# First batch's score limits moved from VectorE to ScalarE, and key splits moved from ScalarE to GpSimd

## The chip, the core and the metric

The kernel runs on one core of a Trainium2 chip. The metric is the device time of one execution in microseconds; the number for the kernel before is the median of three runs. A profiled execution has a span (first to last instruction) and a time of its own, slightly longer.

## What is computed

Three layers follow each other: attention with a threshold, a channel-mixing MLP, and a mixture of experts. Only the first and the start of the second are touched.

```python
scores = scale * np.matmul(q, k.transpose(0, 1, 3, 2))        # 4 batches, 8 heads, 576 x 576, head size 64
thresh = np.max(scores, axis=-1, keepdims=True) - tau
scores = np.where(scores >= thresh, scores, -1000000000.0)
attn = np.exp(scores - np.max(scores, axis=-1, keepdims=True))
attn = attn / (np.sum(attn, axis=-1, keepdims=True) + 1e-09)
x = np.matmul(attn, v)                                        # then: h = x^T U V, u = x + h^T, relu(u w1) w2, experts
```

## The kernel before, in words

**Stages.** Batch 0's attention runs alone (`attention_alone(0)`), beside it only the conversion of the MLP's weights (`convert`), which reads them in 512-column pieces. After it comes a loop over batches 1 to 3, in which the attention of batch b is interleaved with the MLP (`channel`) of batch b - 1. The last MLP and the experts follow.

**Attention.** Two heads are one pair; a batch has four pairs, numbered over all batches i = 4b + hp. A pair has five groups of 128 query rows: four with two score tiles (one for each head) and a fifth with one, so nine score tiles of 128 x 576 in a pair and 36 in a batch. For each score tile the steps are: `scores` (TensorE, four matmuls into a PSUM tile `s`, of which there are two), `peak` (VectorE, the negated row maximum into column 0 of `st`), `exp` (ScalarE, reads `s`, writes `p`), `limits` (column 1 of `st` = row maximum - tau: the lowest score that is kept) and `mask` (VectorE, sets to zero what lies below the limit, and adds up the row in the same instruction). `mask` is the last reader of `s`. Then `back` transposes `p` on TensorE, ScalarE copies the transposed blocks to `ptt`, and matmuls with `v` follow.

**Keys.** Matmuls are done with a high and a low part of each operand. `load_pair` loads a pair's keys in two pieces (576 and 640 columns) into `raw` buffers, of which there are three; `kh` is the rounded copy and `kl` = raw - `kh`. Until now `kh` is always made by ScalarE; `kl` is made by GpSimd (`eng` is `pool`) for pairs 1 to 7 and by VectorE otherwise. A pair's load is issued one pair ahead.

**Order.** Each engine works through its own instructions in order. A scheduler places them, except that GpSimd's stand in the order written while batch 0 runs. SP issues the loads and stores, also in order. `t8` holds the constants from `tau`.

Of the kernel before, what the change touches and what calls it, by code (L numbers as in the profile page):

```python
# [14 lines left out]
AF = mybir.ActivationFunctionType  # L15
ALU = mybir.AluOpType
# [87 lines left out]
def attention_channel_moe(ctx, tc, qk, vv, tau, umat, vrep, wch, wgl, wexp, consts, out):  # L104
    nc = tc.nc
    pe, dve, act, pool, sp = nc.tensor, nc.vector, nc.scalar, nc.gpsimd, nc.sync
# [10 lines left out]
    t8 = cp.tile([128, 4], F32, name="t8")  # L117
# [135 lines left out]
    def scalars():  # L253

        sp.dma_start(out=t8[:, 0:1], in_=tau)

        dve.tensor_scalar(out=t8[:, 1:2], in0=t8[:, 0:1], scalar1=NEGTAU, scalar2=0.125, op0=ALU.is_ge, op1=ALU.mult)
        dve.tensor_scalar(out=t8[:, 2:3], in0=t8[:, 1:2], scalar1=0.0, scalar2=BIG, op0=ALU.is_equal, op1=ALU.mult)
        dve.tensor_scalar(out=t8[:, 0:1], in0=t8[:, 0:1], scalar1=0.0, scalar2=t8[:, 2:3], op0=ALU.max, op1=ALU.add)

    def load_pair(b, hp, later=None):

        i = b * NPAIR + hp
        v = ap.tile([128, VW], F32, tag="v", name=f"v{i}")
        qs = ap.tile([128, QKW], F32R, tag="qs", name=f"qs{i}")
        kh = ap.tile([128, QKW], F32R, tag="kh", name=f"kh{i}")
        kl = ap.tile([128, QKW], F32R, tag="kl", name=f"kl{i}")

        cuts = ((0, 0, 128), (1, 0, S), (0, 704, 832), (1, S, QKW), (0, 128, 704), (0, 832, QKW)) if i == 0 else (
            (1, 0, S), (1, S, QKW), (0, 0, 608), (0, 608, QKW))  # L270
        eng = dve if i == 0 or b > 1 else pool
        def steps():
            for n, (kq, c0, c1) in enumerate(cuts):
                c = slice(c0, c1)
                nm = f"raw{i}_{n}"
                if (i, n) == (0, 1):
                    x = mlp.tile([128, S], F32, tag="yr", name=nm, bufs=2)
                elif i == 0 and c1 - c0 == 128:
                    x = mlp.tile([128, 512], F32, tag="wr", name=nm, bufs=WR)
                else:  # L280
                    x = ap.tile([128, 640], F32, tag="raw", name=nm, bufs=3)
                x = x[:, :c1 - c0]
                sp.dma_start(out=x, in_=qk[i][:, kq, c])
                if (i, n) == (0, 0):
                    scalars()
                if (i, n) == (0, 3):
                    sp.dma_start(out=cst, in_=consts)
                if kq:
                    act.activation(kh[:, c], x, AF.Copy)
                    eng.tensor_tensor(out=kl[:, c], in0=x, in1=kh[:, c].bitcast(F32), op=ALU.subtract)  # L290
                else:
                    act.activation(qs[:, c], x, AF.Copy, scale=t8[:, 1:2])
                    lo, hi, xl = qs[64:128, c], qs[64:128, c].bitcast(F32), x[64:128]
                    dve.scalar_tensor_tensor(out=lo, in0=xl, scalar=t8[64:128, 1:2], in1=hi,
                                             op0=ALU.mult, op1=ALU.subtract)
                yield
            sp.dma_start(out=v, in_=vv[i])

        if later is None:
            for _ in steps():  # L300
                pass
        else:
            later.append(steps())
        return qs, kh, kl, v
# [13 lines left out]
    class Group:  # L318
# [30 lines left out]

        def limits(self, c0, c1):  # L350

            dve.tensor_scalar(out=self.st[:, 1, c0:c1], in0=self.st[:, 0, c0:c1], scalar1=-1.0, scalar2=t8[:, 0:1],
                              op0=ALU.mult, op1=ALU.subtract)

        def halves(self, h):
            return self.pt[:, h].rearrange("p (a b) -> p a b", a=2)
# [1018 lines left out]
```

## Time and profile before

| | us |
|---|---|
| median of 3 runs | 1030.57 (1028.63 to 1031.76) |
| the profiled execution | 1029.61 |
| its span | 1027.8 |
| TensorE busy | 995.2 (97%) |
| VectorE busy | 719.3 (70%) |
| ScalarE busy | 611.8 (60%) |
| GpSimd busy | 152.2 (15%) |

Busy shares are means over all stages. In batch 0's attention alone (up to about 101 us) the shares are others than later, so that stage has to be read by itself. The granted clock of the profiled core was 0.996 over the span.

### The profile page before, as it was taken

How to read it: one execution, taken by the hardware profiler on the slowest of the kernel's cores; microseconds unless marked ns; L12 is line 12 of the kernel's file. 1: busy time of each engine (PE TensorE's matmuls, PEld its weight loads, DVE VectorE, ACT ScalarE, POOL GpSimd, SP SyncE). 2: the span in 40 equal slices, each digit the busy share in tenths (PEclk: the TensorE clock that was granted, in tenths of full speed). 3: DMA queues.
4: the chain of work that ended last, by engine and by line, in shares of the span. 5: the costliest groups of instructions: out<-in, count | busy, mean ns of one | idle time of the engine just before them, and what ended most of it. 6: DMA issues, size and time to landing. Idle time of an engine off the chain costs nothing. (4 is left out here: it accounts for less than half of the span.)

```text
span 1027.8 us, 17859 instructions
## 1 busy us (share of the span) xinstructions
PE 995.2 (97%) x6352; PEld 836.2 (81%) x6352; DVE 719.3 (70%) x1761; ACT 611.8 (60%) x1242; POOL 152.2 (15%) x143
## 2 busy tenths in 40 slices
PE   7898999989999999999999999999999999999996
PEld 4666677768787787788889898999998998889984
DVE  7998697776778877877676664683369755566673
ACT  6888777776677777776565653422354444455562
POOL 1332245342000000000000000013400321120100
PEclk9999999999999999999999999999999999999998
DMA  6655577864323322423121110453055555566550
GB/s 213 220 153 162 160 257 245 273 209 140 116 92 94 125 72 83 127 90 94 55 68 42 42 43 31 139 207 122 25 192 180 177 202 185 174 192 198 196 184 16
DMA packets 58241, 143.72 MB, mean 140 GB/s; under 512 B 7389, under 2 KB 8157, under 8 KB 58144
## 3 DMA queue, kind: packets, MB, share of 16 engines
q1 hardware_dynamic: 54784, 132.27, 40.0%
q0 software_dynamic: 3360, 10.23, 3.1%
q8 instruction: 52, 0.85, 0.3%
q14 instruction: 45, 0.37, 0.1%
HBM read 124.65 MB, written 18.61 MB: 139 GB/s over the span
## 5 line engine op out<-in xcount | busy, mean ns | idle before, releaser
L1125 ACT ACTIVATE eh<-ew 128x512 fp32r<-128x512 f32 x160 | 94.2, 628 | 68.1 <-PE el L1241 47.7
L1126 DVE TENSOR_TENSOR el<-ew,eh 128x512 fp32r<-128x512 f32 x160 | 106.7, 692 | 37.7 <-ACT eh L1125 36.2
L702 PE MATMUL l<-uh,w0h 128*128 128x256 f32 (+2 forms) x352 | 127.0, 361 | 0.3 <-ACT yT L508 0.3
L363 DVE SCALAR_TENSOR_TENSOR p<-s,st,p 128x576 f32<-128x576 f32 x144 | 114.1, 814 | 15.8 <-ACT p L359 12.4
L359 ACT ACTIVATE p<-s,st 128x576 f32<-128x576 f32 x144 | 103.7, 738 | 33.1 <-DVE st L348 31.6
L703 PE MATMUL l<-ul,w0h 128*128 128x256 f32 (+2 forms) x352 | 122.6, 348 | 0.0
L704 PE MATMUL l<-uh,w0l 128*128 128x256 f32 (+2 forms) x352 | 122.3, 348 | 0.0
L348 DVE TENSOR_REDUCE st<-s 128x1 f32<-128x576 f32 x144 | 105.1, 749 | 18.0 <-PE s L315 17.4
L717 PE MATMUL l<-hh,w1h 128*128 128x512 f32 (+3 forms) x320 | 115.2, 360 | 0.0
L719 PE MATMUL l<-hh,w1l 128*128 128x512 f32 (+3 forms) x320 | 112.8, 353 | 0.0
L718 PE MATMUL l<-hl,w1h 128*128 128x512 f32 (+3 forms) x320 | 112.2, 351 | 0.0
L417 ACT ACTIVATE ptt<-tp 128x512 f32<-128x512 f32 (+1 forms) x192 | 88.4, 490 | 30.1 <-PE tp L416 30.0
L313 PE MATMUL s<-kh,qs 128*128 128x288 f32 x320 | 95.5, 318 | 5.6 <-DVE p L363 3.6
L681 POOL TENSOR_TENSOR w1l<-wr,w1h 128x512 fp32r<-128x512 f32 x24 | 31.7, 1333 | 457.5 <-DVE rha L984 426.6
L416 PE MATMUL tp<-cst,p 128*128 128x128 f32 x576 | 90.8, 276 | 5.2 <-ACT ptt L417 5.0
L722 DVE TENSOR_TENSOR yT<-l,yT 128x448 f32<-128x448 f32 (+2 forms) x96 | 50.0, 521 | 57.9 <-PE l L719 57.5
L315 PE MATMUL s<-kl,qs 128*128 128x288 f32 x320 | 88.5, 296 | 0.0
L373 ACT ACTIVATE p<-p,rv 128x576 f32<-128x576 f32 x108 | 78.6, 771 | 15.3 <-DVE rv L380 15.0
L416 PEld LDWEIGHTS tp<-cst,p 128*128 128x128 f32 x576 | 67.8, 140 | 20.6 <-ACT ptt L417 11.4
L313 PEld LDWEIGHTS s<-kh,qs 128*128 128x128 f32 x320 | 60.3, 188 | 15.6 <-DVE p L363 6.4
L435 PE MATMUL po<-ptt,v 128*64 128x256 f32 (+1 forms) x256 | 69.8, 413 | 2.4 <-ACT ptt L424 1.5
L706 DVE SCALAR_TENSOR_TENSOR hl<-l,hh 128x512 fp32r<-128x512 f32 (+2 forms) x80 | 46.3, 578 | 36.7 <-ACT hh L705 36.4
(604 smaller groups left out, 2468.6 us busy)
## 6 DMA issues: line engine op xcount, KB each, us to landing
ew<-in_wexp_dram SPq DMA_DIRECT2D x80, 512.0 KB, 4.6
wr<-wdram SPq DMA_DIRECT2D x128, 256.0 KB, 3.1
cr<-in_wch_dram SPq DMA_DIRECT2D x32, 512.0 KB, 5.2
raw<-in_qk_dram SPq DMA_DIRECT2D x30, 304.0 KB, 3.2
wdram<-w SPq DMA_DIRECT2D x32, 256.0 KB, 3.0
v<-in_vv_dram SPq DMA_DIRECT2D x16, 352.0 KB, 3.9
raw<-in_qk_dram SPq DMA_DIRECT2D x16, 320.0 KB, 3.8
raw<-in_qk_dram SPq DMA_DIRECT2D x17, 288.0 KB, 3.0
```

What stands on the lines that cost most here:

```text
L313: pe.matmul(s["t"][:, h, :288], lhsT=qs[:, qc:qc + 128], rhs=kh[:, k0:k0 + 288], start=(j == 0), stop=False)
L348: dve.tensor_reduce(out=self.st[:, 0, h:h + 1], in_=self.t[h], axis=AX.XY, op=ALU.max, negate=True)
L359: act.activation(self.halves(h), self.t[h], AF.Exp, bias=self.st[:, 0, h:h + 1])
L363: dve.scalar_tensor_tensor(out=p, in0=self.t[h], scalar=self.st[:, 1, h:h + 1], in1=p, op0=ALU.is_ge, op1=ALU.mult, accum_out=self.rvs[:, ...
L416: pe.transpose(tp[:, c - c0], src[:, c * 128:c * 128 + 128], ident)
L702: pe.matmul(pm, lhsT=w1h[:, wk], rhs=uh[k], start=(k == 0), stop=False)
L703: pe.matmul(pm, lhsT=w1h[:, wk], rhs=ul[k], start=False, stop=False)
L704: pe.matmul(pm, lhsT=w1l[:, wk], rhs=uh[k], start=False, stop=(k == 3))
L717: pe.matmul(pm, lhsT=w2h[:, wd], rhs=xh, start=(f == f0), stop=False)
L718: pe.matmul(pm, lhsT=w2h[:, wd], rhs=xl, start=False, stop=False)
L719: pe.matmul(pm, lhsT=w2l[:, wd], rhs=xh, start=False, stop=(f == f0 + 3))
L1126: dve.tensor_tensor(out=lo, in0=x, in1=hi.bitcast(F32), op=ALU.subtract)
```

## The change

Two edits. In batch 0, `limits` is one ScalarE instruction for each score tile (36 in all) in place of one on VectorE; it needs -tau as a bias, which one more VectorE instruction writes to `t8` at the start. And where `kl` is made by GpSimd (pairs 1 to 7, two pieces each, 14 in all), `kh` is made there too, in place of ScalarE.

```diff
@@ scalars
+        dve.tensor_scalar(out=t8[:, 3:4], in0=t8[:, 0:1], scalar1=-1.0, scalar2=None, op0=ALU.mult)
@@ load_pair
                 if kq:
-                    act.activation(kh[:, c], x, AF.Copy)
+                    if eng is pool:
+                        pool.tensor_copy(kh[:, c], x)
+                    else:
+                        act.activation(kh[:, c], x, AF.Copy)
                     eng.tensor_tensor(out=kl[:, c], in0=x, in1=kh[:, c].bitcast(F32), op=ALU.subtract)
@@ Group.limits
-            dve.tensor_scalar(out=self.st[:, 1, c0:c1], in0=self.st[:, 0, c0:c1], scalar1=-1.0, scalar2=t8[:, 0:1],
-                              op0=ALU.mult, op1=ALU.subtract)
+            if self.b == 0:
+                act.activation(self.st[:, 1, c0:c1], self.st[:, 0, c0:c1], AF.Identity, scale=-1.0, bias=t8[:, 3:4])
+            else:
+                dve.tensor_scalar(out=self.st[:, 1, c0:c1], in0=self.st[:, 0, c0:c1], scalar1=-1.0, scalar2=t8[:, 0:1],
+                                  op0=ALU.mult, op1=ALU.subtract)
```

The scheduler sees the new program, so the order shifts on every engine up to the middle of batch 1. Line numbers behind 259 grow by up to 7.

VectorE in batch 0, pair 3, group 2, before (`TENSOR_REDUCE` is `peak`, `TENSOR_SCALAR` on `st` is `limits`, the one that writes `p` is `mask`; the last number of an `s` name is the buffer's):

```order
L348 TENSOR_REDUCE st_3_2_1007<-s_3_2_0_1008 128x1
L379 TENSOR_SCALAR rv_3_0_902<-rv_3_0_902 128x4
L352 TENSOR_SCALAR st_3_2_1007<-st_3_2_1007,t_63 128x1
L380 RECIPROCAL rv_3_0_902<-rv_3_0_902 128x4
L348 TENSOR_REDUCE st_3_2_1007<-s_3_2_1_1027 128x1
L363 SCALAR_TENSOR_TENSOR p_3_2_1006,rv_3_0_902<-s_3_2_0_1008,st_3_2_1007,p_3_2_1006 128x576
L465 TENSOR_TENSOR xsd_0_1_364<-tx_2_4_1046,rv_2_0_632 128x256
L352 TENSOR_SCALAR st_3_2_1007<-st_3_2_1007,t_63 128x1
L363 SCALAR_TENSOR_TENSOR p_3_2_1006,rv_3_0_902<-s_3_2_1_1027,st_3_2_1007,p_3_2_1006 128x576
```

And the same place on VectorE now:

```order
L352 TENSOR_REDUCE st_3_2_1008<-s_3_2_0_1009 128x1
L386 TENSOR_SCALAR rv_3_0_903<-rv_3_0_903 128x4
L387 RECIPROCAL rv_3_0_903<-rv_3_0_903 128x4
L352 TENSOR_REDUCE st_3_2_1008<-s_3_2_1_1028 128x1
L370 SCALAR_TENSOR_TENSOR p_3_2_1007,rv_3_0_903<-s_3_2_0_1009,st_3_2_1008,p_3_2_1007 128x576
L472 TENSOR_TENSOR xsd_0_1_365<-tx_2_4_1047,rv_2_0_633 128x256
L352 TENSOR_REDUCE st_3_3_1073<-s_3_3_0_1074 128x1
L370 SCALAR_TENSOR_TENSOR p_3_2_1007,rv_3_0_903<-s_3_2_1_1028,st_3_2_1008,p_3_2_1007 128x576
```

The two `limits` are gone, and the next tile's `peak` has come ahead of the second `mask`.

ScalarE at the same place now (L366 is `exp`, L357 the new `limits`, L424 copies transposed blocks, L482 scales rows for the channel mixing):

```order
L366 ACTIVATE p_3_2_1007<-s_3_2_0_1009,st_3_2_1008 128x576
L357 ACTIVATE st_3_2_1008<-st_3_2_1008,t_63 128x1
L449 ACTIVATE yT_356<-po_2_4_1001 128x320
L366 ACTIVATE p_3_2_1007<-s_3_2_1_1028,st_3_2_1008 128x576
L424 ACTIVATE ptt_3_0_1038<-tp_3_0_0_1039 128x4x128
L424 ACTIVATE ptt_3_0_1038<-tp_3_0_4_1054 128x4x128
L482 ACTIVATE xsd_0_1_365<-tx_2_4_1047,rv_2_0_633 64x64 x2
L357 ACTIVATE st_3_2_1008<-st_3_2_1008,t_63 128x1
```

29 of the 36 new instructions stand directly behind their `exp`; seven have other work between, here four instructions, two of which (L482) wait for VectorE.

GpSimd from pair 1 to pair 3, now (`CAST` to `kh` is new; before, the same rows stood there without them, and `w0l_0` and `w1l_0` ahead of pair 3's two `kl`):

```order
L291 CAST kh_195<-raw_1_217 128x640
L294 TENSOR_TENSOR kl_196<-raw_1_217,kh_195 128x640
L237 TENSOR_TENSOR vst<-wv_335,vst 32x512 x2
L237 TENSOR_TENSOR vst<-wv_375,vst 32x64 x2
L291 CAST kh_453<-raw_0_455 128x576
L294 TENSOR_TENSOR kl_454<-raw_0_455,kh_453 128x576
L291 CAST kh_453<-raw_1_489 128x640
L294 TENSOR_TENSOR kl_454<-raw_1_489,kh_453 128x640
L291 CAST kh_719<-raw_0_721 128x576
L688 TENSOR_TENSOR w0l_0_1356<-wr_0_0_1353,w0h_0_1355 128x512
L294 TENSOR_TENSOR kl_720<-raw_0_721,kh_719 128x576
```

Each `kl` now stands behind a cast of GpSimd's own in place of a wait for ScalarE.

## Rows read from the trace of the kernel before

**Rows 1.** The page: busy tenths in 40 slices of 25.7 us each.

```profile
PE   7898999989999999999999999999999999999996
DVE  7998697776778877877676664683369755566673
```

**Rows 2.** Busy time by stretch: length, PE, PEld, DVE, ACT, POOL, clock, DMA.

```profile
10.00:101.00 91.00, 79.12 (x555) 58.01 (x555) 84.50 (x202) 73.75 (x154) 25.72 (x20) 1.00 0.60 183
101.00:260.00 159.00, 150.97 (x906) 115.81 (x906) 121.83 (x258) 117.57 (x227) 59.32 (x58) 1.00 0.66 211
260.00:500.00 240.00, 239.33 (x1489) 190.60 (x1488) 180.29 (x453) 169.28 (x346) 0.00 (x0) 1.00 0.31 97
```

**Rows 3.** Waits, 10 to 101 us: total us, times, longest.

```profile
DVE st L348 <- PE s L315: 3.5, 6, 1.2
DVE p L363 <- ACT p L359: 1.2, 2, 0.9
...
PE tp L416 <- ACT ptt L417: 4.0, 6, 1.3
```

**Rows 4.** Groups on DVE, 10 to 101 us: busy us, mean ns, idle before.

```profile
L294 DVE SCALAR_TENSOR_TENSOR qs<-raw,t,qs 64x608 fp32r<-64x608 f32 x9 | 8.4, 934 | 0.3
L219 DVE SCALAR_TENSOR_TENSOR w<-cr,top 128x512 int32<-128x512 int32 x7 | 7.6, 1085 | 0.0
L352 DVE TENSOR_SCALAR st<-st,t 128x1 f32<-128x1 f32 x35 | 6.9, 209 | 0.3
L379 DVE TENSOR_SCALAR rv<-rv 128x4 f32<-128x4 f32 x8 | 3.5, 444 | 0.1
```

**Rows 5.** Timeline of DVE: start, length.

```profile
14.31 0.82 DVE L363 SCALAR_TENSOR_TENSOR p<-s,st,p 128x576 f32<-128x576 f32 x1 [0.24 <-ACT p L359]
...
47.01 0.21 DVE L352 TENSOR_SCALAR st<-st,t 128x1 f32<-128x1 f32 x1
47.14 1.71 DVE L219 SCALAR_TENSOR_TENSOR w<-cr,top 128x512 int32<-128x512 int32 x1
...
81.72 0.85 DVE L294 SCALAR_TENSOR_TENSOR qs<-raw,t,qs 64x608 fp32r<-64x608 f32 x1
...
88.55 0.81 DVE L363 SCALAR_TENSOR_TENSOR p<-s,st,p 128x576 f32<-128x576 f32 x1
```

**Rows 6.** Groups on ACT, 10 to 101 us, as in rows 4.

```profile
L289 ACT ACTIVATE kh<-raw 128x640 fp32r<-128x640 f32 x5 | 3.7, 738 | 0.6 <-DMA raw<-in_qk_dram 0.6
L289 ACT ACTIVATE kh<-raw 128x576 fp32r<-128x576 f32 x5 | 3.4, 681 | 1.4 <-issue 0.8 <-POOL w1l L681 0.6
```

**Rows 7.** Single lines: duration in ns, min/median/max.

```profile
L428 ACT ACTIVATE ptt<-tpr x16: 206/212/227, 38.5 to 617.5; 64x64 f32<-64x64 f32 x16
...
L678 POOL CAST w1h<-wr x14: 605/610/1144, 93.1 to 248.9; 128x512 fp32r<-128x512 f32 x14
...
L379 DVE TENSOR_SCALAR rv<-rv x13: 135/158/1205, 25.5 to 108.7; 128x4 f32<-128x4 f32 x8, 128x1 f32<-128x1 f32 x4, 128x2 f32<-128x2 f32 x1
...
L219 DVE SCALAR_TENSOR_TENSOR w<-cr,top x7: 676/683/1721, 32.0 to 96.4; 128x512 int32<-128x512 int32 x7
```

**Rows 8.** Timeline of ACT.

```profile
13.54 1.37 ACT L359 ACTIVATE p<-s,st 128x576 f32<-128x576 f32 x2
...
41.53 0.51 ACT L475 ACTIVATE xsd<-tx,rv 64x64 f32<-64x64 f32 x2 [1.30 <-DVE xsd L465]
...
87.67 0.74 ACT L359 ACTIVATE p<-s,st 128x576 f32<-128x576 f32 x1
```

**Rows 9.** Timeline of POOL.

```profile
47.03 1.27 POOL L681 TENSOR_TENSOR w0l<-wr,w0h 128x512 fp32r<-128x512 f32 x1 [11.51 <-DMA wr<-wdram]
```

**Rows 10.** Waits of PE, 101 to 260 us.

```profile
PE tx L461 <- ACT yT L442: 2.0, 2, 1.2
```

**Rows 11.** Waits of POOL (0 to 110 us) and of SP's queue (0 to 260 us).

```profile
POOL kl L290 <- ACT kh L289: 18.5, 4, 13.4
...
SPq L283 <- POOL kl L290: 26.8, 11, 9.4
```

## The prediction, as put on record before the changed kernel was run

> **What bounds the kernel now.** I read the page first, for the shape over time: TensorE is at nine tenths or more in nearly every slice, but the first four slices, which are batch 0's attention, have a 7 and two 8s, and there VectorE shows 7, 9, 9, 8 [rows 1]. So I cut the span by stage. From 10 to 101 us VectorE is busy 84.5 of 91 us (93%), ScalarE 73.75 (81%), GpSimd 25.7 (28%). From 260 to 500 us TensorE is busy 239.3 of 240 [rows 2]. The reader should take two things from this. A microsecond that batch 0 loses should be kept to the end, since TensorE runs without pause behind it. And in batch 0 itself TensorE's 79.1 are no limit, although its share looks high: VectorE is the fullest engine.
>
> The waits of that stretch say the same. VectorE's largest wait is 3.5 us in six pieces, for score matmuls; TensorE's largest is 4.0 us for ScalarE's copies of transposed blocks [rows 3]. No wait is large, so nothing but VectorE's own sum of work explains the stage, with ScalarE 11 us behind it. This is a stage of two nearly full engines that hand tiles to each other.
>
> **The change, part by part.** *VectorE loses 36 limits.* 35 of them lie in the stretch (one starts before 10 us), busy 6.9 us, 209 ns each [rows 4]. An instruction's duration overstates what it takes of an engine that overlaps the start of the next: the limit at 47.01 is followed by the next instruction at 47.14, so 0.13 us from start to start [rows 5]. Bounds are 36 x 0.13 = 4.7 and 36 x 0.209 = 7.5 us; I take the middle of the unit costs, 0.165, since some limits stand right behind the reduction that they read and cost more than their issue: 5.9 us less. The one new instruction on `t8` costs about one limit, at the very start, behind a load that is waited for anyway: nothing.
>
> *ScalarE gains 36 small instructions and loses casts.* A limit on ScalarE is 128 x 1, which the trace doesn't have there. The nearest rows are the 64 x 64 copy, 212 ns [rows 7], and the 64 x 64 scaling by a pointer, two in 0.51 us, so about 0.25 each [rows 8]. I take 0.23: 8.3 us (7.6 to 9.2 at the bounds). It loses the ten casts of pairs 1 to 5, 3.7 + 3.4 = 7.1 us [rows 6]. Net +1.2 us on an engine with 17 us idle in the stretch [rows 2]: no cost by its sum. If that idle time weren't there, it would be the 1.2. (The Trainium skill, "ScalarE: Activation LUTs", section "Rules for kernel authors", budgets about 0.3 us for an ACTIVATE with a pointer bias: by it the limits would be an estimated 10.8 us and ScalarE's net 3.7. The two small rows here lie below it.)
>
> *The limit now stands in the chain from exp to mask.* Before, VectorE made it while ScalarE made the exp. Now mask waits for both, on one engine, one behind the other. What this costs depends on how closely mask followed exp. The first close one: the first exp of the pair of them that starts at 13.54 and takes 1.37 us together (so about 0.74 for it) is followed by the mask at 14.31. The last: exp at 87.67 + 0.74 = 88.41, mask at 88.55 [rows 5, 8]. Going through all 36 in this way, 14 masks start within 0.25 us of their exp's end, on average 0.10 behind it; the other 22 have more slack than the limit takes. 14 x (0.23 - 0.10) = 1.8 us lost. Bounds: 0, if the masks' places on VectorE are filled with other work (the new order puts the next tile's reduction there), and 36 x 0.23 = 8.3, if all wait. Behind a waiting mask stand the next reduction, and behind that the next exp, and the score matmuls that need the PSUM tile. Seven limits have other ScalarE work ahead of them; these stand where the order has other VectorE work ahead of the mask, and I count them with the rest.
>
> *GpSimd gains 14 casts, ten of them in batch 0.* A cast of 512 columns takes 0.610 us [rows 7], so 0.69 for 576 and 0.76 for 640 columns: 5 x 1.45 = 7.2 us in batch 0, on an engine that is idle for 65 of 91. GpSimd gets to keys earlier: `kl` now waits 18.5 us in all for ScalarE's `kh`, up to 13.4 at a time, and SP's loads of raw data wait 26.8 us for `kl` [rows 11]. That can only improve, but no engine waits long for keys, so I count nothing. What speaks against the casts is VectorE. The weight join at 47.14 takes 1.71 us while GpSimd works from 47.03 to 48.30 [rows 5, 9], and the same join's median is 0.683 [rows 7]. Over the stretch the seven joins lose 7 x (1.085 - 0.683) = 2.8 us, the eight 128 x 4 scalings 8 x (0.444 - 0.158) = 2.3, the nine query splits 9 x (0.934 - 0.85) = 0.8 [rows 4, 5, 7]: 5.9 us in 25.7 us of GpSimd work, 0.23 per us. 7.2 us of casts would add 1.7; but a cast is half as long as the subtractions, and what meets one waits for less, so I take half, 0.8. Bounds 0 and 7.2 (every cast met for its whole length).
>
> *Batch 1.* ScalarE loses the other four casts, at 0.71 us each 2.8 us; TensorE has 8 us idle from 101 to 260 [rows 2], of it 2.0 us in its largest wait for ScalarE [rows 10]. The casts are few there: 0.5 us less, bounds 0 and 2.8. GpSimd, at 59 of 159 us [rows 2], has the room.
>
> *Sum:* -5.9 + 1.8 + 0.8 - 0.5 = -3.8 us. The profiled execution took 1029.61 us, its span 1027.8, so the new one should take 1025.8. The median of the runs lies 0.96 higher, at 1030.57: I predict 1026.8 us, 0.37% less. A measurement of this kernel can tell about 0.3%, 3.1 us, from no change, so this is close to that bound.
>
> **Rivals.** *All of the relief is kept.* VectorE's order has been rearranged, masks have other work ahead of them, casts cost nothing, and ScalarE's freed time in batch 1 is worth 1.5: -7.4 us, 1023.2. For it: 22 masks have slack. Against it: a fuller share of ScalarE makes slack smaller. Chance 0.15.
>
> *Nothing moves.* Then VectorE's sum wasn't what set batch 0's length, but the round of scores, peak, exp and mask over two PSUM tiles; what VectorE saves comes back as waits for ScalarE, of which it has few now. The longer chain just pays for the shorter sum: 1029 to 1031.5, middle 1030.3. For it: ScalarE is at 81% and its load grows. Against it: VectorE had only 6.5 us idle in 91, so there were hardly any waits of that kind before. Chance 0.23.
>
> *Slower by the longer chain.* Place: ScalarE's queue in batch 0. If each of the 36 masks waits for its limit, with VectorE having worked off all else, the term of 1.8 becomes 8.3: -5.9 + 8.3 + 0.8 - 0.5 = +2.7, 1033.3. It turns slower from about 27 masks that wait in full (27 x 0.23 = 6.2 against 5.9 + 0.5). Chance 0.09.
>
> *Slower by GpSimd.* Each cast blocks VectorE for its whole length: -5.9 + 1.8 + 7.2 - 0.5 = +2.6, 1033.2. For it: the joins of 1.7 us. Against it: GpSimd is busy 28% of the time, and masks and reductions, which read PSUM, are not of the kinds of instruction that lost time (the mask at 88.55 takes 0.81, that at 14.31 0.82 [rows 5]). Chance 0.05. (The Trainium skill, "SBUF — State Buffer", section "SBUF: two separate sides", says that GpSimd and a VectorE instruction with two SBUF inputs, or in a two-port mode, exclude each other for a whole instruction; the join at 47.14 has two such inputs and agrees.)
>
> *The forecast,* part of the relief kept: chance 0.48, its own range 1025 to 1028.5.
>
> **How the numbers follow.** Faster by over 0.3% is below 1027.5: about 0.7 of the forecast's 0.48, and all of the first rival's 0.15, gives 0.49. Slower is the last two, 0.14. The rest, 0.37, is no change that can be told. The range for 8 in 10 reaches from 1021.5 (a little beyond the first rival, 0.15) to 1032.5, which leaves out most of the two slower cases and little below.
>
> **What would show it.** In the profile after: no line of limits on VectorE in batch 0; 36 instructions of 0.2 to 0.25 us on ScalarE; VectorE's busy time up to the last mask of batch 0 lower by 5 to 7 us; the first MLP matmul 3 to 4 us earlier. VectorE's waits before mask for ScalarE, 1.2 us now over the stretch [rows 3], should grow by some 2; if they grow by 6 or more, the second or third rival is right. Joins and scalings on VectorE should lose some 1 us more to GpSimd; with 5 or more the last rival is. If batch 0 ends earlier and the time doesn't follow, the carry to the end was wrong.

## The result and the profile after

The changed kernel is slower: a median of 1041.14 us (1036.77 to 1045.59, 4 runs) against 1030.96 us of the kernel before beside it, ratio 1.0103, 95% interval 1.0079 to 1.0127 (a ratio on record is not the quotient of the two medians, here and below). That is about 10 us the wrong way, and outside the range that I gave. The profiled execution took 1037.71 us, with a span of 1035.8; it is 8.1 us above the profiled one of before.

The page of the changed kernel: TensorE's busy time, then TensorE, its granted clock and VectorE in 40 slices.

```profile
PE 999.5 (96%) x6351; PEld 839.0 (81%) x6352; DVE 712.3 (69%) x1726; ACT 610.8 (59%) x1264; POOL 168.3 (16%) x157
...
PE   7889899999999999999999999999999999999996
...
DVE  6877877686768878786775664583368855566673
...
PEclk8999999999999999999999999999999999999998
```

TensorE is busy for 999.5 us, where its page before has 995.2, with the same work. So in this execution, of the span's 8.0 us, 4.3 are matmuls that took longer, and 3.7 are added idle time. VectorE's first slices, which had 7, 9, 9 and 8 tenths [rows 1], now have 6, 8, 7 and 7: it was relieved as planned.

The windows by stage, columns as in [rows 2]:

```profile
10.00:101.00 91.00, 76.83 (x512) 56.00 (x514) 73.11 (x153) 70.32 (x170) 30.03 (x27) 0.94 0.56 176
101.00:260.00 159.00, 149.44 (x897) 113.97 (x898) 119.26 (x254) 112.04 (x217) 68.59 (x64) 0.99 0.64 210
260.00:500.00 240.00, 239.32 (x1464) 189.33 (x1463) 180.59 (x447) 172.97 (x353) 1.92 (x2) 1.00 0.31 100
```

Batch 0's granted clock is 0.94, where it was 1.00 [rows 2]. In 91 us TensorE got through 512 matmul records in place of 555. From 260 to 500 us it is busy for 239.3 of 240 us, as before. The groups of lines from 10 to 101 us, as in [rows 4]:

```profile
L357 ACT ACTIVATE st<-st,t 128x1 f32<-128x1 f32 x34 | 10.0, 294 | 0.0
...
L291 POOL CAST kh<-raw 128x576 fp32r<-128x576 f32 (+1 forms) x9 | 6.1, 688 | 26.8 <-PE s L317 15.6 <-DMA raw<-in_qk_dram 11.1
...
L219 DVE SCALAR_TENSOR_TENSOR w<-cr,top 128x512 int32<-128x512 int32 x6 | 4.6, 767 | 0.0
```

A limit on ScalarE takes 0.29 us, not 0.23. The joins got shorter (0.767 for 1.085 [rows 4]), so GpSimd's casts don't stand in the joins' way. The waits of 10 to 101 us, as in [rows 3]:

```profile
POOL kh L291 <- PE s L317: 15.6, 2, 12.7
...
DVE st L352 <- PE s L319: 7.4, 11, 1.4
...
PE s L317 <- DVE p L370: 6.3, 4, 2.4
...
PE idle L592 <- ACT ptt L424: 4.7, 2, 4.1
ACT qs L296 <- DMA raw<-in_qk_dram: 3.9, 3, 2.3
DVE p L370 <- ACT st L357: 3.5, 6, 1.8
```

Part of what VectorE was relieved of has come back as waits: 7.4 us for scores (3.5 before) and 3.5 for limits (1.2 for exps before [rows 3]). TensorE has one wait of 4.1 us, and GpSimd waited 12.7 us for old keys to come free. The clock, in windows of 2 us at the start:

```profile
12.00:14.00 2.00, 0.69 (x6) 0.45 (x5) 1.38 (x2) 1.28 (x3) 1.54 (x2) 1.00 0.94 341
14.00:16.00 2.00, 0.95 (x8) 0.95 (x8) 1.76 (x5) 0.95 (x3) 1.07 (x2) 1.00 0.94 349
16.00:18.00 2.00, 1.52 (x8) 1.10 (x6) 1.48 (x3) 1.70 (x4) 1.72 (x2) 0.54 0.08 26
18.00:20.00 2.00, 0.23 (x1) 0.26 (x2) 1.97 (x4) 1.50 (x4) 0.00 (x0) 0.50 0.16 18
20.00:22.00 2.00, 2.00 (x7) 1.49 (x9) 1.22 (x5) 0.10 (x1) 0.00 (x0) 0.50 0.95 327
22.00:24.00 2.00, 2.00 (x13) 1.59 (x13) 1.21 (x3) 2.00 (x5) 0.00 (x0) 0.76 0.31 122
```

Of before, one such window, and TensorE's two pauses:

```profile
20.00:22.00 2.00, 2.00 (x15) 1.43 (x12) 1.94 (x5) 1.98 (x4) 0.00 (x0) 1.00 0.83 265
...
15.19 0.40 PE L313 MATMUL s<-kh,qs 128*128 128x288 f32 x1 [2.18 <-DVE p L363]
...
18.57 0.37 PE L313 MATMUL s<-kh,qs 128*128 128x288 f32 x1 [1.50 <-DVE st L352]
```

TensorE paused from 12.69 to 15.05 us; its clock fell to 0.50, the lower of its two levels (1.2 in place of 2.4 GHz), and a second pause from 17.52 to 19.77 followed. From 20 to 22 us it was busy without a gap, with 7 matmuls; before, the same window held 15 at a clock of 1.00. Before, the same two pauses took 2.18 and 1.50 us, and the clock stayed at 1.00. So the clock had fallen behind a first pause that was only 0.18 us longer, and the second pause came at the low clock already. It falls twice more, at 60 to 64 and 192 to 198 us, each time behind a stall. The first of them, in timelines of GpSimd, SP's queue, ScalarE and TensorE:

```profile
51.80 0.67 POOL L291 CAST kh<-raw 128x576 fp32r<-128x576 f32 x1 [12.72 <-PE s L317]
52.42 1.29 POOL L688 TENSOR_TENSOR w0l<-wr,w0h 128x512 fp32r<-128x512 f32 x1
53.66 1.98 POOL L294 TENSOR_TENSOR kl<-raw,kh 128x576 fp32r<-128x576 f32 x1
...
55.67 5.70 SPq L284 DMA_DIRECT2D raw<-in_qk_dram  x4
...
58.40 0.80 ACT L296 ACTIVATE qs<-raw,t 128x608 fp32r<-128x608 f32 x1 [2.34 <-DMA raw<-in_qk_dram]
...
60.55 0.58 PE L592 MATMUL idle<-idle 128*128 128x512 bf16 x1 [4.09 <-ACT ptt L424]
```

Pair 3's first cast waits for the score matmuls to let go of an older pair's `kh`. A weight subtraction of 1.29 us stands between it and its own subtraction, which ends at 55.64. At that point SP can issue the load of the second query piece, because there are three `raw` buffers and four pieces, and the fourth takes the first one's. ScalarE stands 2.34 us for this piece, with the copies of transposed blocks behind it in its order, and TensorE stands 4.09 us for the copies. Before, the first subtraction of this pair began at 52.42, and the load was issued at 53.85. In batch 1 the same chain gives a pause of 2.39 us that ends at 192.86.

### The profile page after: what moved, and what is told of

The parts are those of the page before. It is cut to its first block, busy times and chain, and to the rows that moved or that the text cites. A ratio compares the mean times of both kernels' runs of the same rounds, so it can differ in the third digit from the quotient of the medians.

```text
span 1035.8 us, 17831 instructions
## 1 busy us (share of the span) xinstructions
PE 999.5 (96%) x6351; PEld 839.0 (81%) x6352; DVE 712.3 (69%) x1726; ACT 610.8 (59%) x1264; POOL 168.3 (16%) x157
## 5 line engine op out<-in xcount | busy, mean ns | idle before, releaser
L366 ACT ACTIVATE p<-s,st 128x576 f32<-128x576 f32 x144 | 103.9, 740 | 36.2 <-DVE st L352 34.8
L424 ACT ACTIVATE ptt<-tp 128x512 f32<-128x512 f32 (+1 forms) x192 | 88.7, 490 | 33.7 <-PE tp L423 33.4
L442 PE MATMUL po<-ptt,v 128*64 128x256 f32 (+1 forms) x256 | 71.6, 420 | 3.9 <-ACT ptt L431 2.4
L443 PE MATMUL po<-ptt,v 128*64 128x256 f32 (+1 forms) x256 | 71.9, 420 | 0.3 <-ACT ptt L424 0.3
```

Source lines behind the costliest of these rows:

```text
L366: act.activation(self.halves(h), self.t[h], AF.Exp, bias=self.st[:, 0, h:h + 1])
```

## The experiments

The theories: **L**, the limit behind exp lengthens the round of a score tile. **Q**, GpSimd gives `raw` back late, the second query piece is loaded late, ScalarE stands with ready copies behind it, TensorE pauses. **C**, behind longer pauses TensorE's clock falls, and the time lost at 1.2 GHz is kept to the end; **P**, only the pauses count. **G**, GpSimd's time itself costs (late weights and keys, contention). **S**, ScalarE, relieved, runs ahead and then stands for loads.

Ratios to the kernel before, run beside each (its median lay at 1030.8 to 1031.4 for e1 to e12, at 1034.7 for e13 to e17, so those go by their ratios). e1 to e8 ran on one chip, e9 to e12 on a second, e13 to e15 on a third, e16 and e17 on a fourth, so runs of different groups are compared by their ratios alone:

| run | what | median us | ratio | 95% interval |
|---|---|---|---|---|
| e1 | limits only | 1036.99 | 1.0060 | 1.0041 to 1.0079 |
| e2 | casts only | 1041.78 | 1.0109 | 1.0083 to 1.0135 |
| e3 | change, query buffer apart | 1041.03 | 1.0084 | 1.0054 to 1.0114 |
| e4 | before, query buffer apart | 1041.47 | 1.0096 | 1.0071 to 1.0120 |
| e5 | limits, 16 fillers | 1031.94 | 1.0010 | 1.0000 to 1.0020 |
| e6 | change, 16 fillers | 1039.01 | 1.0077 | 1.0057 to 1.0097 |
| e7 | before, 16 fillers | 1030.81 | 0.9995 | 0.9980 to 1.0011 |
| e8 | before, early fillers out | 1035.16 | 1.0031 | 1.0017 to 1.0045 |
| e9 | e6, queries first | 1037.73 | 1.0061 | 1.0044 to 1.0079 |
| e10 | e5, casts of batch 0 | 1035.35 | 1.0041 | 1.0023 to 1.0059 |
| e11 | e5, casts of batch 1 | 1035.76 | 1.0049 | 1.0029 to 1.0069 |
| e12 | before, queries first | 1032.70 | 1.0018 | 1.0003 to 1.0033 |
| e13 | e9, 8 fillers more | 1043.82 | 1.0101 | 1.0073 to 1.0129 |
| e14 | e11, batch 1's queries first | 1037.98 | 1.0031 | 1.0015 to 1.0046 |
| e15 | before, useless casts ahead | 1044.10 | 1.0090 | 1.0061 to 1.0119 |
| e16 | before, useless copies behind | 1035.61 | 0.9999 | 0.9985 to 1.0013 |
| e17 | e15, queries first | 1037.99 | 1.0039 | 1.0018 to 1.0060 |

**One part alone (e1, e2).** In e1 the casts go back to ScalarE, in e2 the limits to VectorE:

```diff
e1: -                    if eng is pool:
    +                    if False:
e2: -            if self.b == 0:
    +            if self.b < 0:
```

> The change with its first edit alone: limits of batch 0 on ScalarE, key casts back on ScalarE. Theory Q (the casts free the raw buffers late, the query loads come late, ScalarE stands still behind them in its own order, TensorE idles for 4 us and its granted clock falls): no such stall here, time 1026 to 1033 us, granted clock 1.00 from 56 to 64 us. Rival L (the limit behind each exp makes the loss): slower by 6 us or more, as the full change, with VectorE's waits for limits as the largest.

> The change with its second edit alone: key casts of pairs 1 to 7 on GpSimd, limits back on VectorE. Theory Q: 5 to 12 us slower than before, with ScalarE waiting 2 us or more at a time for a load of raw query data and the granted clock below 1 right after. Rival L: within 2 us of before.

e2 came out as Q said. e1 lies between the two ranges: it loses 5.6 us, where Q had 2 at most and L 6 or more, and VectorE's largest wait is for scores (9.8 us), not for limits (3.5). Each part is slower by itself, so neither theory alone will do; the two don't add up either (0.60 and 1.09% against 1.03%). In e1 the pauses at the start take 2.36 and 2.26 us and the clock is at 0.50 between 16 and 24 us; in e2 the start is that of before, with pauses of 2.18 and 1.50, and the clock first falls at 60 to 65 us, behind a stall for a late query piece.

**Another division of the raw buffers (e3, e4).** Two for keys and one for queries, in the changed kernel and in that of before:

```diff
-                    x = ap.tile([128, 640], F32, tag="raw", name=nm, bufs=3)
+                    x = ap.tile([128, 640], F32, tag="rk" if kq else "rq", name=nm, bufs=2 if kq else 1)
```

> The full change, but of the three raw buffers two are for keys and one is for queries alone, so that no query load waits for GpSimd. Theory Q: the stalls at query loads are gone, and most of the loss with them: 1026 to 1033 us. Rival L: no change against the full change, 1037 us or more.

> The kernel before with the same division of the raw buffers, to see what the division does by itself. Theory Q and rival L: within 3 us of before, 1028 to 1034 us; if it is faster by more, part of what the previous kernel gives is due to the division alone.

Q missed in e3, where L's range held, and e4 missed what both expected. The division alone costs the kernel before 0.96%, so e3 can't tell whether it cured anything. What it does show: this kernel loses 10 us by a change that adds no work at all. That turned me from the work to the pauses and the clock.

**The clock (e5 to e8).** Fillers are matmuls whose result nobody reads; the loop has some already. e5, e6 and e7 add eight behind each of tiles 1 and 3, to the limits alone, to the full change, and to the kernel before. e8 takes the loop's fillers of the first four tiles out of the kernel before:

```diff
e5, e6, e7:
-            turn_over(int((0.8 - spent) / 0.2), i)
+            turn_over(int((0.8 - spent) / 0.2) + {1: 8, 3: 8}.get(i, 0), i)
e8:
+            turn_over(int((0.8 - spent) / 0.2) if i > 3 else 0, i)
```

> The kernel with the limits alone on ScalarE, and eight more filler matmuls on TensorE behind the pieces of tile 1 and of tile 3, so that the two pauses of 2.36 and 2.26 us at 13.3 and 19.0 us are partly filled with work that nobody needs (about 1.5 to 2 us each at 0.25 us a filler). Theory C (the pauses by themselves cost little; the fall of the granted clock to 1.2 GHz behind them makes TensorE slow for some 10 us, and that is kept to the end): the clock stays at 1.00 from 13 to 26 us, and some 3 to 6 us of the 5.6 come back, 1031 to 1034. Theory P (the pauses themselves, that is the longer chain exp, limit, mask, are the loss, and the low clock falls into time that TensorE has over): the clock may stay, but the time doesn't improve, 1036 to 1040.

> The full change with the same sixteen fillers. Theory C: the clock stays at 1.00 at 16 to 24 us, the falls at 60 and 192 us remain, so about a third to a half of the loss comes back, 1034 to 1037. Theory P: no better than the change, 1038 to 1043.

> Control: the kernel before with the same sixteen fillers, where the clock at the start was 1.00 already. Theory C: nothing to gain, and up to 2 us lost where a filler stands ahead of a score matmul, 1030 to 1034, clock 1.00 as before. If the kernel loses 5 us or more with this edit, then any change of the order of batch 0 costs that much, and the two parts of the change have no cost of their own that these runs can tell.

> The kernel before without the loop's filler matmuls for its first four tiles (those ahead of the loop stay). Theory C: the same pauses, without the fillers between them, let the clock fall to 1.2 GHz somewhere from 10 to 26 us, and the kernel loses 3 to 8 us, 1034 to 1039, with none of the change in it. Theory P: VectorE and ScalarE have the same work in the same order, so batch 0 ends as before, 1029 to 1032.

The window of 12 to 26 us, columns as in [rows 2], of e1, e5, e7 and e8 in turn:

```profile
12.00:26.00 14.00, 9.35 (x41) 7.48 (x41) 10.66 (x20) 8.76 (x19) 2.90 (x2) 0.63 0.59 176
```
```profile
12.00:26.00 14.00, 12.26 (x71) 7.93 (x71) 12.48 (x26) 11.36 (x25) 2.96 (x2) 1.00 0.68 217
```
```profile
12.00:26.00 14.00, 13.14 (x79) 8.23 (x78) 13.39 (x34) 11.08 (x20) 2.97 (x2) 1.00 0.72 222
```
```profile
12.00:26.00 14.00, 11.71 (x60) 8.89 (x61) 11.64 (x27) 10.19 (x19) 2.94 (x2) 0.71 0.63 195
```

C is right for the limits, and P falls. With useless work in the pauses the clock stays at 1.00, and 5.0 of e1's 5.6 us come back. The same fillers give the kernel before nothing, where the clock was up already. With its own early fillers taken out the kernel before falls to 0.71 in this window and loses 0.31%, with no part of the change in it. (The scheduler also shifts neighbours in the order, so the runs differ by a little more than the clock. By the traces it is about 10 of VectorE's 1,726 instructions and 16 of ScalarE's 1,278 between e1 and e5, and 26 of 1,761 and 73 of 1,242 between before and e8, whose expectation says that the order is the same.)

e6 missed. The clock is at 1.00 from 12 to 26 us, but only 2.1 of the 10 us came back, with intervals that overlap (1.0077 against 1.0103), and 1039.01 lies in P's range. So with the casts in the kernel the fillers were not shown to help. In its profiled execution the clock stays up behind a pause of 2.04 us that ends at 62.9, and falls to 0.50 behind one of 3.27 that ends at 193.5.

What else e5 says, in its window and waits of 10 to 101 us:

```profile
10.00:101.00 91.00, 82.53 (x558) 57.95 (x559) 75.58 (x161) 79.21 (x187) 25.86 (x20) 1.00 0.58 177
...
DVE st L352 <- PE s L319: 6.5, 12, 1.4
...
DVE p L370 <- ACT st L357: 4.9, 5, 1.4
```

With the clock held, VectorE is busy 75.58 us, 8.9 less than before [rows 2]. Part of this is work that now falls behind the window: from 10 us to the last mask of batch 0 VectorE is busy 75.3 us, where it was 82.5, so the relief is 7.3 us. Yet this mask ends 1.8 us later than before, and the first MLP matmul stands at 114.6 us, 1.3 later. VectorE waits longer for scores (6.5 for 3.5 us) and, where it waited 1.2 us for exps [rows 3], 4.9 for limits.

**The casts by batch (e10, e11).** e6 with the casts on GpSimd in one batch only:

```diff
e10: +                    if eng is pool and b == 0:
e11: +                    if eng is pool and b == 1:
```

> The limits and the sixteen fillers, with the casts on GpSimd in batch 0 alone (batch 1's back on ScalarE). The exps of the run with all casts lag those of the run with none by 3.5 to 4.5 us behind the stall at 61 us and by 9 behind the one at 191 us. Theory Q: only the first of them is left, 1034 to 1036.5. If the casts cost by contention with VectorE, batch 0 with ten of fourteen casts has most of the loss: 1037 to 1039.

> The limits and the sixteen fillers, with the casts on GpSimd in batch 1 alone. Theory Q: the stall at 191 us alone, with the low clock behind it, 5 to 6 us: 1036 to 1038.5. If the loss goes by the number of casts, four of fourteen cost some 2 us: 1033 to 1034.5.

Against e5's 1.0010, ten casts in batch 0 cost 0.31% and four in batch 1 cost 0.39; together, in e6, 0.67. So they add up. By the number of casts it would be 0.48 and 0.19, which the intervals (about 0.2 either way) don't rule out. e10 lies in Q's range; e11 lies a little below it and above that of the count. In e11's profiled execution the clock was 1.00 to 260 us, so the low clock that Q expected there didn't come; in it the pauses alone are the loss.

**The wait for the raw buffer (e9, e12, e14).** The query pieces are loaded ahead of the key pieces, so that no query takes a buffer that this pair's keys still hold (e14 in batch 1 only):

```diff
-            (1, 0, S), (1, S, QKW), (0, 0, 608), (0, 608, QKW))
+            (0, 0, 608), (0, 608, QKW), (1, 0, S), (1, S, QKW))
```

> The full change with the sixteen fillers, and each pair's two query pieces loaded ahead of its two key pieces. With three raw buffers and four pieces a pair, the fourth piece takes the buffer of the pair's first: today that is the second query piece, which so waits until GpSimd is through with cast and subtraction of the pair's first keys. Theory Q (this wait is what the casts cost): the waits of 2.2 and 3.2 us of ScalarE's query scaling at 61.6 and 191.7 us go, and with them TensorE's pauses and the fall of the clock at 192 to 200 us; 1030 to 1034 against 1039.0. Theory G (GpSimd's keys themselves are late for the score matmuls, or the casts stand in the way of VectorE): little comes back, 1036 to 1040, with TensorE waiting for kh or kl.

> Control: the kernel before with the query pieces loaded first. Its query scaling waits 0.8 us at most for raw data, so there is little to win by it: 1028 to 1033 if the order of the loads is harmless in itself; 1035 or more if it takes more than it gives, which would have to be taken off the reading of the run with queries first.

> The limits, the sixteen fillers and the casts on GpSimd in batch 1 alone, with batch 1's queries loaded first. Without that order the clock stayed at 1.00 and 3.8 us were lost, with a TensorE pause of 1.76 us at 188.8 behind a query scaling that waited 1.7 us for its data. Theory Q: that pause goes, 1032 to 1034.5. Theory G (GpSimd later with the next weights and keys, many small waits): 1035 to 1037.

e9 missed Q's range and lies in G's: it gave back 0.16% against e6, with intervals that overlap, though the waits named in its expectation went. ScalarE's query scaling waited 0.7 us for data in all, and no TensorE pause of 0.9 us or more was for keys, as G would have it. The order itself costs 0.18% (e12), and a new pause of 1.43 us at 35.8 us, behind a weight block that ScalarE waited for, was followed by 1.2 GHz to 44 us. e14 has 0.31% where e11 had 0.49, with intervals that overlap; that is 3.2 us, within Q's range. The direction is Q's; these three runs don't decide.

**More fillers for e9 (e13).** Eight at tile 10, ahead of that pause.

```diff
-            turn_over(int((0.8 - spent) / 0.2) + {1: 8, 3: 8}.get(i, 0), i)
+            turn_over(int((0.8 - spent) / 0.2) + {1: 8, 3: 8, 10: 8}.get(i, 0), i)
```

> The full change with the sixteen fillers and the queries loaded first, and eight more fillers behind the pieces of tile 10, ahead of the pause of 1.43 us at 35.8 us behind which the clock stood at 1.2 GHz from 37 to 44 us. Theory C: the clock stays at 1.00 there, and 2 to 4 us of the 5.8 come back, 1033.5 to 1035.5. If no more than 1 us comes back (1036.5 or more), the clock isn't what is left of the casts' cost, but the pauses themselves and GpSimd's work.

Missed. The clock held from 34 to 44 us, but the kernel got slower, which by the expectation counts against the clock as what is left of the casts' cost. ScalarE's timeline has a new stall:

```profile
73.34 0.63 ACT L687 ACTIVATE w1h<-wr 128x512 fp32r<-128x512 f32 x1 [4.95 <-DMA wr<-wdram]
```

Behind it TensorE paused 3.46 us, and the clock fell to 0.50 at 76. So filling one pause doesn't cure the casts: the next load is waited for somewhere else.

**GpSimd's work by itself (e15 to e17).** To tell G, Q and S apart I left ScalarE's casts where they were and gave GpSimd fourteen useless ones. In e15 each stands ahead of its subtraction, into the tile that the subtraction then writes, and so holds `raw` for longer. In e16 the same number stands behind, when `raw` is free. e17 is e15 with the queries first.

```diff
e15, e17:
+                    if eng is pool:
+                        pool.tensor_copy(kl[:, c], x)
                     eng.tensor_tensor(out=kl[:, c], in0=x, in1=kh[:, c].bitcast(F32), op=ALU.subtract)
e16:
                     eng.tensor_tensor(out=kl[:, c], in0=x, in1=kh[:, c].bitcast(F32), op=ALU.subtract)
+                    if eng is pool and n == 1:
+                        for q in (slice(0, S), slice(S, QKW)):
+                            pool.tensor_copy(kl[:, q], kl[:, q].bitcast(F32))
```

> The kernel before, ScalarE's casts as they were, and fourteen useless casts more on GpSimd: each of the key pieces of pairs 1 to 7 is first cast to the low part's tile, which the subtraction then overwrites. Theory G: GpSimd's 9.4 us more, and what they delay (subtraction, raw buffer, second query piece), are what the casts cost: 1034 to 1038, whether ScalarE is relieved or not. Theory S (what costs is that ScalarE, relieved, runs its order earlier and then stands for loads with ready copies behind it): 1030 to 1033.

> The kernel before with fourteen useless copies on GpSimd, as many and as large as the casts, but behind each pair's subtractions in batch 0: the finished low part is copied onto itself, when the raw buffer is already free (pairs 1 to 3; in batch 1 one of two stands ahead of the second subtraction). Every other engine's order is unchanged. Theory Q (the raw buffer that GpSimd gives back late, and the second query piece behind it): little is lost, 0 to 3 us, ratio below 1.003. Theory G (GpSimd's time itself: contention with VectorE, weights and low parts later): as much as with the casts ahead of the subtraction, ratio 1.006 or more.

> The kernel before with the fourteen useless casts ahead of the subtractions, which cost 0.90%, and the queries loaded first, which by itself cost 0.18%. Theory Q: the second query piece no longer waits for GpSimd, and the sum comes to 0.2 to 0.5%. Theory G: 0.7% or more.

e15 loses 0.90%, about as much as the whole change and more than its expectation gave, with ScalarE not relieved at all: S falls. e16 has the same work on GpSimd, with every other engine's order unchanged, and loses nothing: G, as GpSimd's time itself, falls. (e15's expectation counts the late buffer to G as well; e16 and e17 part the two.) e17 gets more than half of e15's loss back. Both came out as Q said. One rival has no run of its own, the order: e15 is a new program for the scheduler, and by the traces about 64 of VectorE's 1,761 instructions and 45 of ScalarE's 1,242 stand elsewhere than before, in e16 none. The chain in e15's timelines of GpSimd, SP's queue, ScalarE and TensorE:

```profile
32.75 0.66 POOL L291 CAST kl<-raw 128x576 fp32r<-128x576 f32 x1
33.50 1.95 POOL L292 TENSOR_TENSOR kl<-raw,kh 128x576 fp32r<-128x576 f32 x1
...
35.47 0.33 SPq L283 DMA_DIRECT2D raw<-in_qk_dram  x1
...
38.69 0.80 ACT L294 ACTIVATE qs<-raw,t 128x608 fp32r<-128x608 f32 x1 [2.62 <-DMA raw<-in_qk_dram]
...
39.81 0.48 PE L437 MATMUL po<-ptt,v 128*64 128x320 f32 x1 [2.65 <-ACT ptt L425]
```

And before:

```profile
34.01 0.33 SPq L283 DMA_DIRECT2D raw<-in_qk_dram  x1
...
35.63 0.38 ACT L423 ACTIVATE ptt<-tp 128x256 f32<-128x256 f32 x1
...
37.12 0.80 ACT L292 ACTIVATE qs<-raw,t 128x608 fp32r<-128x608 f32 x1 [0.83 <-DMA raw<-in_qk_dram]
```

With one cast ahead the load is issued 1.46 us later, the wait is 1.8 us longer, and TensorE pauses 2.65 us. Two things made this pause: the late piece, and the new order, since before the copies that TensorE waits for stood ahead of this scaling. In batch 1 the order is no rival: from 130 us on to 770 every engine has the order of before, but for GpSimd's casts. There a pair's two casts stand ahead of its first subtraction, and the same chain follows. Before, then e15:

```profile
183.49 0.81 ACT L292 ACTIVATE qs<-raw,t 128x608 fp32r<-128x608 f32 x1 [0.81 <-DMA raw<-in_qk_dram]
...
186.15 0.48 PE L435 MATMUL po<-ptt,v 128*64 128x320 f32 x1 [0.68 <-ACT ptt L424]
```
```profile
192.58 0.80 ACT L294 ACTIVATE qs<-raw,t 128x608 fp32r<-128x608 f32 x1 [2.91 <-DMA raw<-in_qk_dram]
...
195.24 0.80 PE L437 MATMUL po<-ptt,v 128*64 128x320 f32 x1 [2.76 <-ACT ptt L426]
```

Here TensorE's matmuls, 7.0 us later than before ahead of the pause, are 10.3 later behind it. So in this execution the late piece costs 3.3 us at this place with no change of the order, the low clock behind the pause included. In the changed kernel's execution they go from 5.7 to 8.8 there. Behind the first of e15's pauses the clock falls, in its windows:

```profile
40.00:42.00 2.00, 2.00 (x13) 1.01 (x12) 0.84 (x4) 1.72 (x5) 0.00 (x0) 0.77 0.95 305
42.00:44.00 2.00, 2.00 (x9) 1.03 (x5) 0.79 (x3) 0.00 (x0) 0.00 (x0) 0.50 0.81 312
```

ScalarE's waits for query data from 10 to 260 us, in e15, e16 and e17 in turn (4.6, 7 times, longest 0.9 before):

```profile
ACT qs L294 <- DMA raw<-in_qk_dram: 7.4, 5, 2.9
```
```profile
ACT qs L295 <- DMA raw<-in_qk_dram: 5.9, 7, 2.0
```
```profile
ACT qs L294 <- DMA raw<-in_qk_dram: 0.2, 1, 0.2
```

e16 waits for almost as long in all as e15 and loses nothing, so the sum of these waits doesn't give the loss: it depends on where they stand and on what stands behind them.

## Why the prediction was wrong

**VectorE's sum of work as the stage's length.** "Nothing but VectorE's own sum of work explains the stage" was the first step that failed. The relief came (e5: 7.3 us less busy up to the last mask), and with the clock held it was worth nothing: 1.0010. By e5's longer waits for scores and limits, the round of scores, peak, exp, limit and mask set the pace, as in my rival *nothing moves* (1030.3; e5 measured 1031.94 beside a before of 1031.18). The terms of -5.9 and +1.8 measured +0.8 together, and +1.1 against e7, the kernel before with the same fillers. The evidence that I read as VectorE's limit, few waits in a full engine, held only until it had less to do.

**TensorE's 79.1 us "are no limit".** TensorE's speed did count, once the clock fell. Every price in my sum was a price at a granted clock of 1.00, since [rows 2] shows nothing else. I didn't ask what longer pauses (2.36 and 2.26 us for 2.18 and 1.50) may do to TensorE's speed behind them. In e1 this is 5.0 of 5.6 us. Both rivals on the slower side had other mechanisms; none had the clock.

**The limit's cost on ScalarE.** 0.289 us median, above my bounds of 0.21 to 0.25. By the Trainium skill, "ScalarE: Activation LUTs", section "Rules for kernel authors", it would be about 0.3, as an estimate: the Trainium skill was right, and my nearest rows were not near enough. From start to start a limit took 0.19 us of ScalarE behind an exp (13.84 to 14.03), so for ScalarE's sum the size mattered little.

**Keys: "That can only improve, but no engine waits long for keys, so I count nothing."** This was the costliest step. I looked at how long `kl` waits for ScalarE's `kh`, and concluded that a cast on GpSimd makes it earlier. But GpSimd works in order, so the casts lie in its own chain ahead of the subtraction, and the subtraction is what gives `raw` back. [rows 11] had the row: SP's loads waited 26.8 us for `kl`. I named them and didn't follow which piece of data stood behind that wait: the second query piece, then ScalarE's copies, then TensorE. The terms for the casts (+0.8 for contention, -0.5 in batch 1) measured +7.1 us with the clock held at the start (e6 against e5). The contention with VectorE that I did price didn't show: the joins got shorter, and e16 loses nothing with the same GpSimd work, although its interval (0.15% either way) could hide the 0.8 us.

**Carry to the end.** This held: the MLP matmul that stood at 258 us before is 8.4 us late in the changed kernel, and the one that stood at 744 us is 8.6 us late.

**What I said would show it.** VectorE's busy time from 10 us to the last mask of batch 0 fell by 5.5 us (82.5 to 77.0), within the 5 to 7 that I gave, but the first MLP matmul came 5.8 us later (113.28 to 119.07), not 3 to 4 earlier; the waits for ScalarE before mask grew by 2.3, near the 2 I gave, and the joins got shorter.

**Two slips in the sums.** The middle of 0.13 and 0.209 is 0.17, not 0.165. And with the +0.8 left in, the kernel turns slower from 25 masks that wait in full (5.6 / 0.23), not 27. Neither would have changed the forecast.

**Still open.** What makes the clock fall: the length of a pause alone doesn't tell it (last section). How much of the loss in batch 0, in e15 and in the change, is the new order and how much the late query piece; e15's work in the order of before was not run there. Why curing the wait for queries gave back so little in the change itself (e9). Why the two parts together cost no more than the casts alone. What is left in e17 above e12 (0.39 against 0.18%, intervals that overlap). Why e13's weight block came so late. And no version here beats the kernel before; e5, e7 and e16 can't be told from it.

## What to carry to other kernels

Before work is moved to an idle engine, follow the buffer that this work holds: who refills it, which datum comes next through it, and what stands behind the instruction that waits for that datum. Where TensorE has pauses of a microsecond or two, look at the granted clock in small windows behind them, and price a longer pause with the slow time that may follow; useless matmuls in the pause are a cheap test (here they took away the limits' loss alone: see e6 and e13). And try a full engine's relief with the clock held before you believe that its sum was the limit.

## What was unexpected of the hardware

The same pauses don't always have the same clock behind them. In e16, whose other engines' order is that of the kernel before, the profiled execution had the pause of 2.18 us at the start as before, and then 0.50 from 18 to 22 us, where the profiled one of before had 1.00. Over 33 runs of the kernel before on one chip (beside e1 to e8) the mean granted clock went from 0.992 to 0.998, and the time with it: a median of 1033.2 us in the nine runs at 0.993 or less, 1030.0 in the seven at 0.997 or more. The changed kernel's runs do the same: 1036.77 and 1037.71 us at 0.991, 1044.57 and 1045.59 at 0.986 and 0.984.
